# Attention and gated unit on one core: every step in a new written order, batch 0's q turned in row pairs, buffers given by number, ten more fillers on TensorE

## The chip, the core and the metric

The kernel runs on one core of a Trainium2 chip, in one launch. The metric is device time in microseconds (us), lower is better. All data are float32; the three weights of the gated unit arrive as float64 and are narrowed on the core.

## What is computed

The reference, cut to what matters (8 batches, 8 heads, 576 tokens, 64 numbers per head; model width 512; 5 taps):

```
kv   = einsum('bhsd,bhse->bhde', k, v)            # no softmax
out  = einsum('bhsd,bhde->bhse', q, kv)
x    = out / sqrt(mean(out*out, -1) + 1e-6) * g_norm      # then heads side by side: (8, 576, 512)
gate = sigmoid(sum over 5 taps of conv_w[tap] * x shifted by tap)
y    = (gate * (x @ w_val)) @ w_out
```

## The kernel before

The kernel has no loops of its own. A string `PLAN` names 1235 steps with their arguments, and the last lines of the kernel call one small function for each step, in that order. Each function issues a few instructions on a fixed engine, so the string is the order of every engine's queue at once: TensorE (PE) for products, VectorE (DVE), ScalarE (ACT), GpSimd (POOL), and SyncE (SP) for most of the transfers. An engine works its own list in order and waits at the first instruction whose operands are not there. The framework adds the waits.

One batch goes through these steps:

- `load_half k|v b i` (L302) and `load_q`, `load_q_rows` (L313, L327) fetch. For batch 0 the v halves and one half of q go out on ACT's queue, the rest on SP's.
- `turn_q_rows b j` (L471, batches 0 and 1): q lies token by token, and the products need it with the 64 numbers of a head along the partitions. A product with the identity turns one row of 64 numbers for four heads; two of these (upper and lower four heads, r = 0, 1) go to the two halves of the output's partitions. j counts groups of four rows of tokens, and the fifth group has two, so a batch takes 36 such products. `sort_q` (L481) copies the turned rows from the PSUM bank to `qT`, with ACT. Later batches use VectorE's own transpose instead (`turn_q`).
- `kv_product b i` (L432): k times v for half i, 36 products of 64x64. `kv_copy` (L445) puts the sums into SBUF; for batch 0 into the blocks of a block-diagonal matrix `kv_bd`, four copies with ACT.
- `raw_whole` (batch 0, L506) or `raw_pair`, `raw_tail`: q times kv, chunk by chunk of 128 tokens.
- `square` (ACT), `sums` (DVE, a reduction), `powers` (POOL, the inverse root), `normalise` (DVE for batch 0, ACT later): the root-mean-square norm.
- `turn_x`, `keep_x` (PE, ACT), or later `turn_blocks`, `move_blocks` (DVE, then transfers): x with the width along the partitions, in `xT`.
- `gate_start` (ACT), four `gate_tap` (DVE), `gate_end` (ACT, sigmoid), `gated` (DVE): the gate. `val_product` and `keep_val` for batches 0 and 1, `x_sums`, `val_fast` and `val_keep` for the rest: x times w_val. `token_sums`, `fast_product`, `fast_keep` and `out_product`, `keep_out`: the last product; `store` writes.

Beside batch 0, `narrow_weight` turns each 64-bit weight block into float32 in eight steps (five on DVE, three on ACT). `w_val` has four blocks, `w_out` four, and the taps with g_norm one (`cw`); `turn_cw` (PE, L412) and `keep_cw` (DVE, L416) finish the last. `start_warm 36` (L427) gives PE 36 small products with the identity before q arrives; nothing reads them.

Buffers come from rotating pools: a name such as `ot` has three, and each new tile takes the next one. PSUM has eight banks in one rotation:

```
def ps(shape, name):
    return psum.tile(shape, FP32, tag="bank", bufs=8, name=name)
```

Of the kernel before, what the change touches and what calls it, by code (L numbers as in the profile page):

```python
# [10 lines left out]
U32 = mybir.dt.uint32  # L11
# [8 lines left out]
load_q_rows 0 1; stage_weight cw 0; load_q_rows 0 0; load_half v 0 0; load_half k 0 0; narrow_weight cw 0 5;  # L20
narrow_weight cw 0 6; narrow_weight cw 0 0; load_half v 0 1; load_half k 0 1; narrow_weight cw 0 1;
narrow_weight cw 0 2; warm_up; stage_weight wval 1; stage_weight wval 0; start_warm 36; turn_q_rows 0 3;
turn_q_rows 0 2; turn_q_rows 0 0; kv_product 0 0; turn_q_rows 0 1; sort_q 0 0; sort_q 0 1; narrow_weight cw 0 3;
narrow_weight cw 0 4; narrow_weight cw 0 7; turn_q_rows 0 4; turn_cw; keep_cw; kv_product 0 1; sort_q 0 4;
sort_q 0 3; kv_copy 0 0; kv_copy 0 1; narrow_weight wval 1 5; narrow_weight wval 1 0; sort_q 0 2; raw_whole 0 3;
load_q_rows 1 1; narrow_weight wval 1 1; narrow_weight wval 1 6; narrow_weight wval 1 2; raw_whole 0 4;
raw_whole 0 2; load_q_rows 1 0; narrow_weight wval 0 0; narrow_weight wval 0 5; square 0 3; stage_weight wval 3;
narrow_weight wval 0 6; narrow_weight wval 1 3; sums 0 3; load_half k 1 0; square 0 2; square 0 4;
narrow_weight wval 0 1; narrow_weight wval 1 4; sums 0 2; narrow_weight wval 0 2; raw_whole 0 0; raw_whole 0 1;
powers 0 3; sums 0 4; narrow_weight wval 1 7; normalise 0 3; square 0 1; square 0 0; sums 0 1; sums 0 0;  # L30
turn_q_rows 1 2; turn_q_rows 1 0; turn_q_rows 1 3; narrow_weight wval 0 3; sort_q 1 0; turn_x 0 3;
turn_q_rows 1 4; sort_q 1 2; turn_q_rows 1 1; keep_x 0 3; narrow_weight wval 3 0; load_half v 1 0;
stage_weight wval 2; load_half k 1 1; load_half v 1 1; powers 0 2; sort_q 1 3; normalise 0 2;
narrow_weight wval 3 1; narrow_weight wval 0 4; normalise 0 4; narrow_weight wval 0 7; narrow_weight wval 3 5;
stage_weight wout 1; load_q 2 0; stage_weight wout 0; powers 0 1; turn_x 0 4; narrow_weight wval 3 2;
turn_x 0 2; load_half k 2 0; kv_product 1 0; load_q 2 2; stage_weight wout 2; normalise 0 0; normalise 0 1;
narrow_weight wval 3 3; keep_x 0 2; keep_x 0 4; narrow_weight wval 3 4; narrow_weight wval 2 0; turn_x 0 0;
narrow_weight wval 3 6; turn_x 0 1; val_product 0 1 1; keep_x 0 0; kv_product 1 1; keep_x 0 1;
narrow_weight wval 3 7; narrow_weight wval 2 5; gate_start 0 0; val_product 0 3 1; gate_start 0 3;
narrow_weight wval 2 1; halo 0; sort_q 1 4; kv_copy 1 1; sort_q 1 1; kv_copy 1 0; gate_start 0 1;  # L40
narrow_weight wval 2 2; raw_pair 1 3; gate_tap 0 0 3; gate_tap 0 0 2; gate_tap 0 3 3; narrow_weight wval 2 3;
gate_tap 0 3 2; gate_tap 0 0 1; narrow_weight wout 1 0; narrow_weight wout 1 5; narrow_weight wval 2 6;
narrow_weight wval 2 4; load_half v 2 0; load_half k 2 1; load_q 2 1; square 1 3; narrow_weight wout 1 1;
narrow_weight wout 1 2; raw_tail 1; load_half v 2 1; keep_val 0 1 1; val_product 0 0 0; square 1 2;
narrow_weight wval 2 7; keep_val 0 3 1; gate_tap 0 3 1; sums 1 3; gate_tap 0 0 0; narrow_weight wout 0 0;
gate_tap 0 1 3; sums 1 2; turn_q 2 0; powers 1 3; keep_val 0 0 0; gate_end 0 0; val_product 0 2 1;
val_product 0 0 1; powers 1 2; load_q 2 3; narrow_weight wout 1 3; square 1 4; normalise 1 3; sums 1 4;
narrow_weight wout 1 6; narrow_weight wout 1 4; gate_tap 0 1 2; keep_val 0 0 1; val_product 0 1 0; raw_pair 1 1;
normalise 1 2; powers 1 4; turn_x 1 3; square 1 0; val_product 0 2 0; narrow_weight wout 1 7; gated 0 0;
gate_tap 0 1 1; keep_val 0 1 0; normalise 1 4; narrow_weight wout 0 1; sums 1 0; gate_start 0 2; turn_x 1 4;  # L50
turn_x 1 2; val_product 0 3 0; square 1 1; keep_x 1 4; keep_x 1 3; keep_x 1 2; narrow_weight wout 0 5;
gate_tap 0 3 0; val_sums 0; narrow_weight wout 2 5; narrow_weight wout 2 0; powers 1 0; gate_tap 0 2 3;
gate_tap 0 2 2; narrow_weight wout 0 2; gate_tap 0 2 1; sums 1 1; narrow_weight wout 0 3; keep_val 0 2 0;
keep_val 0 3 0; keep_val 0 2 1; stage_weight wout 3; narrow_weight wout 0 4; narrow_weight wout 0 6;
gate_tap 0 1 0; narrow_weight wout 2 6; gate_end 0 3; kv_product 2 0; normalise 1 0; powers 1 1;
val_product 1 0 1; halo 1; val_product 1 1 1; kv_product 2 1; turn_x 1 0; normalise 1 1; keep_val 1 0 1;
turn_q 2 2; narrow_weight wout 0 7; gate_tap 0 2 0; gate_end 0 1; gate_end 0 2; val_sums 1; turn_q 2 1;
gated 0 3; gated 0 2; turn_x 1 1; val_product 1 3 1; load_q 3 0; keep_x 1 0; turn_q 2 3; load_q 3 1;
load_half v 3 0; load_half v 3 1; narrow_weight wout 2 1; kv_copy 2 1; keep_x 1 1; weight_sums 0; val_sums 2;
gate_start 1 1; val_product 1 1 0; kv_copy 2 0; keep_val 1 1 1; narrow_weight wout 2 2; gate_tap 1 1 3;  # L60
keep_val 1 3 1; narrow_weight wout 2 3; narrow_weight wout 3 0; raw_pair 2 3; narrow_weight wout 3 5;
gate_tap 1 1 2; gated 0 1; square 2 2; square 2 3; keep_val 1 1 0; gate_start 1 0; narrow_weight wout 3 1;
raw_pair 2 1; val_product 1 0 0; narrow_weight wout 3 2; val_product 1 3 0; narrow_weight wout 3 3;
narrow_weight wout 3 6; token_sums 0 0 0; sums 2 3; val_product 1 2 1; val_product 1 2 0; powers 2 3; sums 2 2;
turn_q 3 0; token_sums 0 0 1; narrow_weight wout 3 4; square 2 1; keep_val 1 0 0; keep_val 1 3 0; load_q 3 3;
narrow_weight wout 3 7; narrow_weight wout 2 4; narrow_weight wout 2 7; load_half k 3 0; load_q 3 2;
load_half k 3 1; powers 2 2; fast_product 0 0 0; sums 2 1; normalise 2 3; token_sums 0 0 2; turn_blocks 2 3;
normalise 2 2; square 2 0; turn_q 3 1; powers 2 1; gate_start 1 3; fast_product 0 1 0; fast_product 0 0 1;
fast_keep 0 0 0; keep_val 1 2 0; normalise 2 1; weight_sums 1; raw_tail 2; sums 2 0; gate_tap 1 0 3;
fast_keep 0 0 1; fast_product 0 0 2; fast_keep 0 0 2; powers 2 0; square 2 4; keep_val 1 2 1; fast_keep 0 1 0;  # L70
weight_sums 2; token_sums 0 0 3; fast_product 0 0 3; fast_product 0 0 5; turn_blocks 2 2; turn_blocks 2 1;
sums 2 4; fast_keep 0 0 5; gate_tap 1 0 2; normalise 2 0; fast_product 0 0 4; fast_product 0 1 2; powers 2 4;
fast_keep 0 1 2; store 0 0; normalise 2 4; turn_blocks 2 0; move_blocks 2 0; move_blocks 2 2; move_blocks 2 1;
kv_product 3 0; fast_keep 0 0 4; turn_q 3 2; gate_tap 1 0 1; gate_tap 1 0 0; weight_sums 3; turn_q 3 3;
fast_product 0 1 4; turn_x 2 4; fast_product 0 1 1; kv_product 3 1; keep_x 2 4; kv_copy 3 0; kv_copy 3 1;
fast_product 0 0 6; move_blocks 2 3; raw_pair 3 3; raw_pair 3 1; gate_tap 1 3 3; load_half v 4 0; load_q 4 0;
gate_end 1 0; fast_keep 0 1 1; square 3 3; fast_keep 0 0 6; square 3 1; fast_product 0 1 3; fast_product 0 1 5;
gate_tap 1 3 2; gated 1 0; fast_keep 0 1 4; gate_tap 1 1 1; val_fast 2 0 0; sums 3 3; sums 3 1; gate_tap 1 1 0;
fast_keep 0 1 5; square 3 0; fast_product 0 1 6; square 3 2; sums 3 2; x_sums 2 0; gate_end 1 1; val_fast 2 1 0;
powers 3 3; x_sums 2 1; x_sums 2 3; gate_tap 1 3 1; gate_tap 1 3 0; val_fast 2 0 1; val_keep 2 0 0;  # L80
val_fast 2 0 2; x_sums 2 2; val_sums 3; sums 3 0; gated 1 1; fast_keep 0 1 6; val_keep 2 1 0; normalise 3 3;
val_keep 2 0 2; powers 3 2; powers 3 1; gate_end 1 3; val_fast 2 1 2; val_fast 2 1 1; load_half k 4 0;
val_keep 2 1 2; gate_start 1 2; val_keep 2 0 1; val_fast 2 0 4; gate_tap 1 2 3; val_keep 2 1 1; gate_tap 1 2 2;
val_fast 2 1 4; val_fast 2 0 5; val_fast 2 1 5; load_half v 4 1; normalise 3 2; load_half k 4 1; val_keep 2 0 4;
turn_blocks 3 2; val_keep 2 1 4; turn_q 4 0; val_keep 2 1 5; store 0 1; load_q 4 1; store 0 3; gate_tap 1 2 1;
# [763 lines left out]
```

## Time and profile before

| What | Value |
|---|---|
| Runs | 306.4, 304.68, 305.18 us; median 305.18 |
| Profiled execution, span from first to last instruction | 304.6 us |
| PE busy | 294.8 us, 97%, 3441 matmul records |
| DVE busy | 269.2 us, 88%, 474 instructions |
| ACT, POOL busy | 193.7 us (64%), 114.9 us (38%) |
| HBM read, written | 39.21 MB, 9.44 MB |

The profile doesn't say which of the runs, if any, is the profiled one; what lies around its span isn't recorded. The span is 0.1 us under the fastest run and 0.6 us under the median.

How to read it: a float32 product on PE shows as two matmul records, a transpose as one. "Busy" of PE counts a record's whole latency, so neighbours overlap, and the distance from one to the next tells the rate. The chain of waits is followed back from the last instruction; where it stays on PE, PE was never kept waiting. The granted clock (PEclk) is known only from the first clock record on; ahead of that the page prints full.

### The profile page before, as it was taken

To read this page: it belongs to the slowest core of one execution; us is meant where nothing else is said; L and a number is where in the kernel's file an instruction comes from. 1 tells how busy PE (TensorE), PEld (TensorE's weight loads), DVE (VectorE), ACT (ScalarE), POOL (GpSimd) and SP (SyncE) were. 2 spreads that over 40 slices of the span, in tenths; PEclk is the share of its full clock that TensorE was granted. 3 is DMA by queue.
4 is the path that set the end of the run, shared out by engine and by line. 5 is a ranking of instruction groups with operands and counts; after the bars stand their busy time and mean duration, and the time that the engine had idled before them with its cause. 6 is when DMAs were issued, how large, how long until landed. Compare 5 with 4: busy or idle time off the path is not lost.

```text
span 304.6 us, 8977 instructions
## 1 busy us (share of the span) xinstructions
PE 294.8 (97%) x3441; PEld 232.4 (76%) x3441; DVE 269.2 (88%) x474; ACT 193.7 (64%) x596; POOL 114.9 (38%) x127
## 2 busy tenths in 40 slices
PE   7899999999999999999999999999999999999993
PEld 7788778877787785777778757787878588888582
DVE  1169999999999999999999999999999999999612
ACT  1569989999768664884586547683787354535220
POOL 3027354406568217364338352345536631000000
PEclk9979999999999999999999999999999999999999
DMA  7999998088569756988689477927411621112423
GB/s 269 343 368 343 272 302 210 4 230 269 154 147 329 231 163 167 269 220 260 173 253 294 111 175 232 326 72 214 114 48 30 169 80 34 36 42 64 103 69 103
DMA packets 32074, 55.53 MB, mean 182 GB/s; under 512 B 6166, under 2 KB 14358, under 8 KB 32032
## 3 DMA queue, kind: packets, MB, share of 16 engines
q1 hardware_dynamic: 29520, 49.76, 55.7%
q0 software_dynamic: 1632, 3.17, 4.1%
q10 hardware_dynamic: 880, 2.03, 1.8%
q8 instruction: 27, 0.44, 0.6%
q14 instruction: 15, 0.12, 0.1%
HBM read 39.21 MB, written 9.44 MB: 160 GB/s over the span
## 4 chain that ended last, share of the span: by engine, by line
PE 89%; DVE 5%; DMA 2%; issue 1%; ACT 1%; DVEq 0%; ACTq 0%; SPq 0%
PE a L774 18%; PE cb L774 14%; PE va L682 13%; PE val L633 11%; PE vc L682 6%; PE kvps L440 6%; PE raw L501 5%; PE out L720 5%; PE vb L682 4%; PE qTps L477 4%; PE raw L512 2%; PE xTps L583 2%; DMA qs<-in_q_dram 2%; DVE gate L621 2%; DVE xs L667 1%
## 5 line engine op out<-in xcount | busy, mean ns | idle before, releaser
L552 POOL TENSOR_TENSOR rt<-ss,mhalf 128x8 f32<-128x8 f32 (+3 forms) x38 | 68.9, 1822 | 101.0 <-DVE ss L544 100.8
L621 DVE SCALAR_TENSOR_TENSOR gate<-xT,cwT,gate 128x576 f32<-128x576 f32 x128 | 101.8, 809 | 1.0
L571 ACT ACTIVATE x<-raw,rt 128x64 f32<-128x64 f32 x252 | 55.8, 351 | 7.2 <-POOL rt L552 4.2
L604 POOL DMA_DIRECT2D xT<-y x48 | 26.4, 557 | 25.5 <-DVE ot L784 14.0
L633 PE MATMUL val<-xT,wval 128*128 128x288 f32 x128 | 33.0, 411 | 0.0
L774 PE MATMUL a<-wsum,sums 128*128 128x256 f32 x128 | 32.4, 382 | 0.0
L628 ACT ACTIVATE gate<-gate 128x576 f32<-128x576 f32 x32 | 22.0, 692 | 11.7 <-DVE gate L621 11.4
L633 PEld LDWEIGHTS val<-xT,wval 128*128 128x128 f32 x128 | 23.5, 190 | 6.5 <-ACT xT L590 0.4
L544 DVE TENSOR_REDUCE ss<-sq 128x8 f32<-128x520 f32 (+1 forms) x40 | 24.7, 627 | 2.9 <-ACT sq L531 2.5
L774 PEld LDWEIGHTS a<-wsum,sums 128*128 128x128 f32 x128 | 24.0, 190 | 4.1 <-issue 0.6
L535 ACT ACTIVATE sq<-raw 128x256 f32<-128x256 f32 (+1 forms) x70 | 22.4, 403 | 7.3 <-PE raw L501 7.1
L682 PE MATMUL va<-xs,vsum 128*128 128x288 f32 x96 | 26.6, 409 | 0.0
L615 ACT ACTIVATE gate<-xT,cwT 128x576 f32<-128x576 f32 x32 | 25.2, 811 | 1.5 <-DVE gv L646 1.3
L646 DVE TENSOR_TENSOR gv<-gv,gate 128x576 f32<-128x576 f32 x32 | 23.6, 750 | 0.9 <-ACT gate L628 0.8
L682 PEld LDWEIGHTS va<-xs,vsum 128*128 128x128 f32 x96 | 18.0, 190 | 5.1 <-ACT x L571 0.4
L611 POOL COPY xT<-xT 128x124 f32<-128x124 f32 x32 | 17.5, 585 | 10.5 <-ACT xT L590 10.5
L501 PEld LDWEIGHTS raw<-kv,qT 64*64 64x64 f32 x1008 | 16.4, 134 | 5.3 <-issue 3.0
L440 PEld LDWEIGHTS kvps<-v,k 64*64 64x64 f32 x1008 | 15.9, 135 | 3.7 <-issue 1.9
L501 PE MATMUL raw<-kv,qT 64*64 64x64 f32 x1008 | 18.7, 221 | 0.0
L440 PE MATMUL kvps<-v,k 64*64 64x64 f32 x1008 | 17.6, 220 | 0.0
L774 PE MATMUL cb<-wsum,sums 128*128 128x256 f32 x64 | 16.9, 386 | 0.1
L774 PE MATMUL cb<-wout,gv 128*128 128x256 f32 x64 | 16.8, 385 | 0.0
(111 smaller groups left out, 542.3 us busy)
## 6 DMA issues: line engine op xcount, KB each, us to landing
qs<-in_q_dram SPq DMA_DIRECT2D x96, 140.0 KB, 4.2
out_dram<-ot SPq DMA_DIRECT2D x140, 64.0 KB, 1.7
k<-in_k_dram SPq DMA_DIRECT2D x14, 576.0 KB, 6.3
v<-in_v_dram SPq DMA_DIRECT2D x12, 576.0 KB, 6.5
xT<-y SPq DMA_DIRECT2D x48, 64.0 KB, 2.7
xT<-y POOLq DMA_DIRECT2D x48, 64.0 KB, 3.3
y<-in_moe_w_val_dram SPq DMA_DIRECT2D x4, 512.0 KB, 11.4
w_wout<-in_moe_w_out_dram SPq DMA_DIRECT2D x4, 512.0 KB, 6.3
```

The costliest lines, as they stand in the source:

```text
L440: nc.tensor.matmul(st["kvps", b][s][r * D:(r + 1) * D, i], st["k", b, i][rows, r, cols], st["v", b, i][rows, r, cols], start=(j == 0), sto ...
L501: nc.tensor.matmul(st["raw", b, c][r][cols, to * D:(to + 1) * D], st["qT", b][rows, hp, first:first + D], kvs[b % 2][rows, hp, :], start=T ...
L544: nc.vector.reduce_sum(out=st["ss", b][:, FIRST[c]:FIRST[c] + n], in_=st["sq", b, c][:, 0:n], axis=AX.X)
L552: nc.gpsimd.tensor_tensor(out=st["rt", b][:, which], in0=st["ss", b][:, which], in1=mhalf[:, which], op=ALU.pow)
L571: nc.scalar.activation(out=x[:, to * D:(to + 1) * D], in_=raw[:, h * D:(h + 1) * D], func=AF.Copy, scale=root[:, to:to + 1])
L604: (nc.sync if i % 2 else nc.gpsimd).dma_start(out=xTs[b % 2][i * TB:(i + 1) * TB, :, first:first + P], in_=y[a * TB:(a + 1) * TB, i])
L615: nc.scalar.activation(out=gate[:], in_=xTs[b % 2][:, jt, HALO:SX], func=AF.Copy, scale=cwT[:, K - 1, jt:jt + 1])
L621: nc.vector.scalar_tensor_tensor(out=gate[:], in0=xTs[b % 2][:, jt, tap * TB:tap * TB + S], scalar=cwT[:, tap, jt:jt + 1], in1=gate[:], op ...
L633: nc.tensor.matmul(val[:], wval[:, kc, jt * P:(jt + 1) * P], xTs[b % 2][:, kc, HALO + n * SV:HALO + (n + 1) * SV], start=(kc == 0), stop=( ...
L646: nc.vector.tensor_tensor(out=both, in0=both, in1=st["gate", b, jt][:], op=ALU.mult)
L682: nc.tensor.matmul(st[bank, "val", b, mj][:], weights_[:, k], tokens()[:, k], start=(n in (0, 1, 3) and k == 0), stop=(k == NK // 2 - 1), ...
L774: nc.tensor.matmul(st[bank, i, p], tokens()[:, k], weights_[:, k], start=(n < 2 and k == 0), stop=(k == NK // 2 - 1), skip_group_check=True)
```

## The change

The diff replaces the whole string `PLAN` (1235 steps by 1238; the same steps with the same arguments, but for `start_warm`), and it does this in the functions:

- Buffers are no longer pools. Each name has fixed tiles (`ROOMS`), and a step says after an @ which of them its new tiles take. Names and sizes are those of before.
- Batch 0's q is turned by two rows of tokens at a time with a real transpose (128 numbers, two rows of 64, become 128 partitions), 18 instead of 36 operations. The result has the two rows on the two halves of the partitions, so `sort_q` of batch 0 has four copies instead of one, two with ACT and two with DVE.
- `kv_copy` of batch 0 gives two of its four copies to DVE.
- `start_warm` has a width: 36 products of 38 columns instead of 32 before q arrives, and 3, 6 and 1 of 256 columns further on.

By the built programs, PE goes from 1745 products to 1737 (36 row products out, 18 transposes and 10 fillers in), DVE from 476 instructions to 488, ACT from 598 to 601.

The string's beginning, before and after, and the functions:

```diff
-load_q_rows 0 1; stage_weight cw 0; load_q_rows 0 0; load_half v 0 0; load_half k 0 0; narrow_weight cw 0 5;
-narrow_weight cw 0 6; narrow_weight cw 0 0; load_half v 0 1; load_half k 0 1; narrow_weight cw 0 1;
-narrow_weight cw 0 2; warm_up; stage_weight wval 1; stage_weight wval 0; start_warm 36; turn_q_rows 0 3;
-turn_q_rows 0 2; turn_q_rows 0 0; kv_product 0 0; turn_q_rows 0 1; sort_q 0 0; sort_q 0 1; narrow_weight cw 0 3;
-narrow_weight cw 0 4; narrow_weight cw 0 7; turn_q_rows 0 4; turn_cw; keep_cw; kv_product 0 1; sort_q 0 4;
-sort_q 0 3; kv_copy 0 0; kv_copy 0 1; narrow_weight wval 1 5; narrow_weight wval 1 0; sort_q 0 2; raw_whole 0 3;
...
+load_q_rows 0 1; load_q_rows 0 0; load_half v 0 1 @ 0; load_half k 0 1 @ 0; start_warm 36 38 @ 0;
+load_half v 0 0 @ 0; load_half k 0 0 @ 0; stage_weight wval 1; stage_weight wval 0; stage_weight cw 0 @ 0;
+turn_q_rows 0 4 @ 1; turn_q_rows 0 1 @ 0; turn_q_rows 0 2 @ 2; turn_q_rows 0 3 @ 3; turn_q_rows 0 0 @ 4;
+start_warm 3 256 @ 5; load_q_rows 1 1; load_q_rows 1 0; narrow_weight cw 0 5 @ 0; narrow_weight cw 0 0 @ 0;
+stage_weight wval 3; kv_product 0 1 @ 6 7; narrow_weight cw 0 6 @ 1; narrow_weight cw 0 1; load_half k 1 1;
+narrow_weight cw 0 2; load_half v 1 1; warm_up; sort_q 0 4 @ 0; sort_q 0 2; start_warm 6 256 @ 5; sort_q 0 1;
+stage_weight wout 1 @ 1; narrow_weight cw 0 3; narrow_weight cw 0 4; narrow_weight cw 0 7; sort_q 0 0;
+sort_q 0 3; stage_weight wval 2; kv_product 0 0; turn_cw @ 4; start_warm 1 256 @ 5; load_half v 1 0;
+kv_copy 0 0; kv_copy 0 1; narrow_weight wval 1 5 @ 1; raw_whole 0 3 @ 3; narrow_weight wval 1 0 @ 0;
...
+    ROOMS = {"w64": (3, 1024), "ot": (3, 512), "wexp": (2, 512), "gate": (3, 576), "xs": (4, 576), "x": (2,
...
+    def new(tag, shape, dtype, name):
+        room = rooms[tag][picked.pop(0)]
...
     def ps(shape, name):
-        return psum.tile(shape, FP32, tag="bank", bufs=8, name=name)
+        return new("bank", shape, FP32, name)
...
-    def start_warm(n):
+    def start_warm(n, width):
+        reps = -(-width // P)
+        bank = ps([TB, reps, width // reps], f"warm{n}")
         for _ in range(n):
-            nc.tensor.matmul(warm_bank()[0:TB, 0, 0:TB], ident[:, 0:TB], ident[:, 0:TB], start=True, stop=True)
+            nc.tensor.matmul(
+                bank[0:TB], ident[:, 0:TB], ident[:, 0:width // reps].unsqueeze(1).broadcast_to((P, reps, width // reps)),
+                start=True, stop=True)
...
     def kv_copy(b, s):
         ps_ = st["kvps", b][s]
         if b in WHOLE:
             for r in range(2):
                 rows = slice(r * D, (r + 1) * D)
-                nc.scalar.copy(
+                (nc.vector.tensor_copy if r else nc.scalar.copy)(
...
     def turn_q_rows(b, j):
         m = min(HB, NB - j * HB)
-        pq = ps([P, HB, P], f"qTps{b}_{j}")
+        st["pq", b, j] = pq = ps([P, HB, P], f"qTps{b}_{j}")
+        if b in PAIRED_Q:
+            for r in range(2):
+                for n in range(0, m, 2):
+                    nc.tensor.transpose(
+                        pq[:, r * 2 + n // 2, :],
+                        qs[:, r, j * HB + n:j * HB + n + 2, :].rearrange("p n d -> p (n d)"), ident[:])
+            return
...
     def sort_q(b, j):
...
+        if b not in PAIRED_Q:
+            nc.scalar.copy(out=qT[:, j * HB:j * HB + m], in_=pq[:, 0:m])
+            return
+        for r in range(2):
+            for e in range(2):
+                (nc.vector.tensor_copy if b == 0 and e else nc.scalar.copy)(
+                    out=qT[r * D:(r + 1) * D, j * HB + e:j * HB + m:2],
+                    in_=pq[e * D:(e + 1) * D, r * 2:r * 2 + m // 2])
```

`PAIRED_Q` is (0,). Of batch 1 only the order changes.

## Prediction

> **What bounds it now.** I read the page's first and fourth part, then sums over stretches, then the chain's beginning in order of time.
>
> ```profile
> PE 294.8 (97%) x3441; PEld 232.4 (76%) x3441; DVE 269.2 (88%) x474; ACT 193.7 (64%) x596; POOL 114.9 (38%) x127
> ...
> PE 89%; DVE 5%; DMA 2%; issue 1%; ACT 1%; DVEq 0%; ACTq 0%; SPq 0%
> ```
>
> PE is the chain. By stretches (columns: stretch, then busy time and count of PE, PEld, DVE, ACT, POOL; then clock, DMA share, GB/s):
>
> ```profile
> 15.84:22.80 6.96, 6.40 (x84) 5.51 (x76) 4.47 (x10) 5.14 (x12) 1.87 (x1) 0.75 1.02 386
> 22.80:284.00 261.20, 260.31 (x3049) 204.12 (x3049) 256.44 (x432) 179.86 (x567) 110.64 (x118) 1.00 0.62 177
> 23.50:299.60 276.10, 275.10 (x3112) 214.42 (x3112) 261.24 (x440) 182.21 (x574) 110.40 (x117) 1.00 0.60 171
> ```
>
> From 23.5 to 299.6 PE stands idle for 1.0 us in all, and DVE, up to 284, for under 5. Both are full, so the new order can win little there. What is left is the beginning:
>
> ```profile
> 6.12 5.05 PE qTps L477 x48
> 11.17 1.21 PE kvps L440 x72
> 12.38 1.49 PE qTps L477 x24
> 13.86 1.19 issue
> 15.05 0.21 PE cwps L414
> 15.26 1.28 PE kvps L440 x67
> ...
> 17.15 6.32 PE raw L512 x40
> 23.47 2.77 PE qTps L477 x48
> ...
> 30.30 1.02 PE xTps L583 x8
> 31.32 1.70 PE val L633 x7
> ```
>
> Two things are to be seen. PE waits 1.2 us at 13.86 for the taps, and 0.6 more ahead of raw. And equal work takes two lengths: 48 records of q's turning 5.05 us at 6.12, 2.77 us at 23.47. The first are at half clock (105 against 58 ns a record), though the page prints full there, where no clock record exists. The later drop is on record (columns: stretch, PE, clock, DMA, GB/s):
>
> ```profile
> 10.50:13.90 3.40, 3.34 (x107) 1.00 1.06 377
> 13.90:17.30 3.40, 1.69 (x74) 1.00 0.77 253
> 17.30:20.80 3.50, 3.50 (x18) 0.51 1.01 374
> ```
>
> PE half idle for 3.4 us, then half clock for 3.4 us: that made raw 1.7 us longer.
>
> **What doesn't change.** The steps are the same, so PE's dense work is. Each step between 64x64 products (kv, raw) and whole-array ones costs PE 0.18 to 0.2 us (L774 x4 takes 1.06 us behind kv, 0.86 behind its like); both lists have 29 such blocks. Fixed buffers add no instruction; a wait that they add or remove counts in the last term below.
>
> **The beginning, step by step.** Times are on the profile's scale.
>
> *Transfers.* q lands at 6.1 and 6.25. The two k and v halves are only swapped: v lands 8.3 and 12.1 us after issue at 1.2 and 1.7, so 9.5 and 13.8; k's second at 13.6. SP's next loads, batch 1's q, waited for q's turning and went out at 13.88; then DMA ran at 0.77 of its time (row above). Now they can go at about 8.5, so what follows lands some 1 us earlier. w_val, k and v of batch 1 keep ahead of their uses; I take 0 for them.
>
> *Turning.* 36 products, 6.5 us with both clocks, become 18 transposes at 0.11 to 0.13 us (8 in 1.02), 2.0 us at full clock. The warm-up of 38 columns runs 38/32 as long as the old (4.05 us), 4.8, so to about 6: next to no gap ahead of q, where 0.7 us stood. With PE busy from 1.4 on I take full clock from about 7, so turning ends at 8.6. Three fillers of 256 columns (0.43 each, L774) end at 9.9, kv 0 1 at 11.2, six fillers at 13.8, just as k and v land; kv 0 0 at 15.1, `turn_cw` and the last filler at 15.7. So the fillers cost nothing if the clock is up. If it isn't, they push kv back (the second rival).
>
> *Copies.* ACT: 10 copies, 0.25 to 0.3 each; it is free of the table load at 11.2 and through with them and the taps' third step at about 14.2. DVE: 10 copies of 64x256 from PSUM. No row has one; 0.33 (L784's 256-column pace) is one end, 0.42 (L797 alone) the other: 3.3 to 4.2 us, of which six lie in a stretch that was idle (8.45 to 14.36: 5.25 us in one wait). The other four sit behind `narrow_weight cw 0 7`, which waits for ACT, at 13.8: through at 15.1 to 15.5. I take 0.33, the pace of a full queue. Behind those DVE has two kv copies, then w_val's narrowing, for which everything later waits. kv's four copies took 1.09 us on ACT alone; in twos beside each other 0.5. So raw starts at 15.7 instead of 17.15, and DVE at 15.6 instead of 15.84. Bounds: 15.6 to 16.3.
>
> *Raw to the first val.* Raw takes 4.45 at full clock (records 112 ns apart at its end), so to 20.15, against 23.47: 3.3 us gained. DVE's list, added up in its new order, stays fed: narrowing 5 steps and `keep_cw` to 18.5, then sums and narrowing by turns (0.60, 0.34, 0.65, 0.70 each); x of chunk 3 at 22.2, 4 at 25.0, 2 at 25.6, 0 and 1 at 28.2 and 28.8. In the old list 2.6 us of waits for `square` stood between 15.84 and 23. PE now comes first at the turning of x: its waits there are 0.3, 0.4 and 0.6. With turning (2.8 + 1.5), kv 1.4, x 2.0 the first val begins at 29.5, against 31.32. **The lead is 1.8 us**, not 3.3: DVE has the rest.
>
> *Later.* DVE gains once more. A `gate_tap` right behind one on the same gate waits for its result (first row: two gates; second: one gate):
>
> ```profile
> 272.42 1.54 DVE L621 SCALAR_TENSOR_TENSOR gate<-xT,cwT,gate 128x576 f32<-128x576 f32 x2
> ...
> 280.44 1.66 DVE L621 SCALAR_TENSOR_TENSOR gate<-xT,cwT,gate 128x576 f32<-128x576 f32 x2
> ```
>
> 0.12 us each. Instructions of DVE that read the one just ahead of them: 50 in the old list, 32 in the new, so 2.2 us less on DVE. That is cover for PE, not time: PE has only its 1.0 us of idle time, and some restarts behind it, to win. I take 0.4 of that. New waits at other places can cost: from 0 up to one whole handoff from square to x (0.58 + 0.70 + 2.06 + 0.68 = 4.0, rows L531, L544, L552, L561); I take 0, as DVE's lead over PE has grown, and keep both ends. The tail behind `out_product 3 8` has the same 26 half products and stores: 0.
>
> **Sum.** 304.6 - 1.8 - 0.4 = 302.4 on the profiled execution's scale. The median of the runs lies 0.6 higher, so 302.9.
>
> **Rivals.**
>
> *All of DVE's lead arrives.* DVE's 2.9 us at the start (2.6 of waits, 0.24 of start) and all idle time of PE: 304.6 - 2.9 - 1.0 = 300.7, 301.2 as a median. For it: DVE is full. Against: PE has no such slack.
>
> *The fillers run at half clock: slower.* The clock was still half at 10.5 in the old kernel, with 72 warm-up records and some 40 of q behind it; transposes may do still less to raise it. Then turning takes 3.8 us (to 10.0), three fillers 2.6 (to 12.6); with full clock from 13.9, one stretch of 3.4 us of products later, kv 0 1 ends at 14.5, the six fillers, which now stand in front of k and v that have landed, at 17.1, kv 0 0 at 18.5, and raw begins at 19.0. Raw ends where it did (23.45), but DVE's narrowing starts 3.3 us later than I forecast, so the first val comes at 32.8, 1.4 later than before: 306.0, 306.4 as a median. It decides when full clock comes after about 11.5; later than 13.9, up to 1 us more. The Trainium skill (TensorE: Matmul & The Clock Gate, part 4, PE-mode transpose) says that transposes don't count as work for the clock; by that rule this rival holds. No run yet shows a stretch of them.
>
> *The lead is lost later.* An order is only as good as the times it was planned with. A handoff 1.8 us short, under half of the 4.0 chain, uses it up: 304.6, 305.1 as a median. For it: PE and DVE are both full, so nothing makes up for it. Against: DVE's extra 2.2 us.
>
> *It does not do what it says.* The fillers are real work for PE, as the lists show, so this could only be the clock, above.
>
> **Chances.** Forecast 0.45 (302.9, spread about 1 us), DVE's whole lead 0.12, lost later 0.23, half-clock fillers 0.20. About 0.5% (1.5 us, 303.7 and 306.7) is what a measurement can tell from no change. Faster: 0.12 and five sixths of 0.45, 0.50. Same: the rest of the forecast, the lost lead, and half of the fillers' case, 0.36 with a little off for worse handoffs. Slower: 0.14. The range takes in both ends: 300.9 to 306.4.
>
> **What would show it.** Full clock ahead of the first kv and none below it until the end; kv 0 0 at about 13.8; raw at 15.7, 4.45 us long; w_val's narrowing at 15.6 and DVE without a wait for `square`; the first val at 29.5. Wrong, if kv 0 0 starts behind fillers after k and v have landed, if PE waits for DVE between 30 and 284 by more than 1 us, or if DVE has idle time there while PE is busy with what it waits for.

## The result, and the profile after

| | before | after |
|---|---|---|
| Median of 6 runs each (lowest to highest) | 305.47 us (304.68 to 306.4) | 315.58 us (313.98 to 317.85) |
| Ratio | | 1.034 [1.030, 1.038] |
| Span of the profiled execution | 304.6 us | 314.5 us |
| First val product begins | 31.32 us | 32.65 us |
| PE idle from raw's end to the end of its dense work | 1.0 of 276.1 us | 9.6 of 285.7 us |

Slower by 10 us, where 2.3 faster was forecast. Two rows hold it all: the first val product comes 1.3 us later, and PE then stands idle for 8.6 us more. 1.3 + 8.6 = 9.9, the difference of the spans. Before's trace is that of its longest run (306.4 us; every run with both numbers lies about 1.8 us above its span), after's that of a run 0.7 us above the median.

The page of after, the lines that answer to the first ones of before (busy time, and the chain of waits by engine):

```profile
PE 296.4 (94%) x3407; PEld 231.8 (74%) x3407; DVE 272.0 (86%) x486; ACT 195.9 (62%) x599; POOL 112.7 (36%) x127
...
PE 54%; DMA 17%; DVE 14%; SPq 8%; issue 3%; ACT 2%; POOL 1%; DVEq 0%; POOLq 0%; ACTq 0%
```

PE's busy share fell only from 97 to 94%, but the chain left PE: from 89% to 54%. DMA, DVE and SP's issuing (SPq) now hold 39% of it. That is how a kernel looks whose busiest engine is kept waiting. By stretches (stretch; busy time and count of PE, PEld, DVE, ACT, POOL; granted clock, DMA share, GB/s):

```profile
6.20:8.50 2.30, 2.24 (x19) 2.07 (x20) 0.26 (x2) 0.00 (x0) 0.00 (x0) 1.00 1.05 398
...
14.60:18.20 3.60, 1.46 (x35) 0.86 (x33) 2.64 (x9) 1.89 (x7) 0.00 (x0) 1.00 1.02 387
...
18.70:22.10 3.40, 3.40 (x20) 3.18 (x20) 3.27 (x10) 2.46 (x5) 0.00 (x0) 0.50 1.06 387
...
24.40:310.10 285.70, 276.06 (x3112) 215.40 (x3112) 259.39 (x439) 183.55 (x573) 108.04 (x117) 1.00 0.57 163
```

The transposes of q (first row) run at full clock: it is granted from 5.04 us on. Then PE works for 1.46 of 3.6 us, and half clock follows for 3.4 us, as it did before; raw again takes 6.2 us. The last row is the dense stretch, with its 9.6 us of idle time.

The beginning's chain in order of time (start, length, what; the numbered buffers make every PSUM tile a "bank"):

```profile
13.94 0.37 ACT qT L531
14.31 0.02 issue
14.33 0.43 DVE qT L531
...
16.16 0.43 DVE qT L531
16.58 0.03 issue
16.61 0.44 DVE qT L531
17.05 0.02 issue
17.07 0.37 ACT qT L531
17.45 0.02 issue
17.47 0.43 DVE qT L531
17.90 0.22 DVE kvbd L484
18.11 0.04 issue
18.16 6.22 PE bank L559 x40
...
32.65 0.49 PE bank L680 x2
```

`sort_q`'s copies (L531) of one bank run in single file: ACT, DVE, ACT, DVE. Only the first copy of a bank runs beside the last one of the bank ahead (four times in 20 copies). So raw (L559) starts at 18.16, later than the old 17.15, and not at 15.7.

What PE waited for, in all (us in total, times, longest):

```profile
PE bank L729 <- DMA xT<-y: 2.2, 2, 1.4
PE bank L474 <- DMA qs<-in_q_dram: 2.2, 1, 2.2
PE bank L474 <- issue: 1.4, 1, 1.4
...
PE bank L729 <- ACT x L618: 1.2, 1, 1.2
PE bank L820 <- DVE ot L830: 0.9, 1, 0.9
PE bank L474 <- DMA k<-in_k_dram: 0.8, 1, 0.8
PE bank L820 <- ACT ot L834: 0.7, 1, 0.7
...
PE bank L820 <- ACT ot L836: 0.6, 1, 0.6
```

No single wait is the loss. Transfers (x's moves, k and v) stand for 5.2 us of it, `ot` for 2.2. L474 is the kv product, which reads k and v and not q: at 107 it waits for semaphores 103 and 108, which v (issued at 99.37) and k (issued at 102.30, landed at 108.83) raise; a q load is on one of the two as well, which is how the wait got its name. In the chain:

```profile
92.53 0.77 SPq L356
93.30 0.05 issue
93.36 6.00 DMA qs<-in_q_dram
99.36 0.02 issue
99.37 5.21 DMA v<-in_v_dram
104.58 0.02 issue
104.60 4.38 DMA qs<-in_q_dram
108.98 1.27 PE bank L474 x72
```

From 93.36 on one transfer follows another with 0.02 us between them, all on SP's list (the last, too, is k and not q). In the trace SP's transfers go round eight semaphores, and one waits until the last one on its semaphore, most often eight issues earlier, has landed. k's issue stood behind a q load that waited until 101.47 for the v load of 94.74. A load of k takes 6.5 us to land (median), so a load that stands behind others goes out late however free its buffer is.

### The profile page after: what moved, and what is told of

Read it like the earlier page. It is cut to its first block, busy times and chain, and to the rows that moved or that the text cites. A ratio compares the mean times of both kernels' runs of the same rounds, so it can differ in the third digit from the quotient of the medians.

```text
span 314.5 us, 8915 instructions
## 1 busy us (share of the span) xinstructions
PE 296.4 (94%) x3407; PEld 231.8 (74%) x3407; DVE 272.0 (86%) x486; ACT 195.9 (62%) x599; POOL 112.7 (36%) x127
## 4 chain that ended last, share of the span: by engine, by line
PE 54%; DMA 17%; DVE 14%; SPq 8%; issue 3%; ACT 2%; POOL 1%; DVEq 0%; POOLq 0%; ACTq 0%
PE bank L820 17%; PE bank L729 12%; PE bank L680 10%; DMA qs<-in_q_dram 6%; DMA v<-in_v_dram 4%; PE bank L474 4%; DVE gate L668 4%; PE bank L767 3%; SPq L852 3%; DMA xT<-y 3%; PE bank L548 3%; SPq L651 2%; PE bank L559 2%; DVE gv L693 2%; DMA w<-in_moe_conv_w_dram 2%
## 5 line engine op out<-in xcount | busy, mean ns | idle before, releaser
L668 DVE SCALAR_TENSOR_TENSOR gate<-xT,cwT,gate 128x576 f32<-128x576 f32 x128 | 100.5, 808 | 0.6
L618 ACT ACTIVATE x<-bank,rt 128x64 f32<-128x64 f32 x252 | 56.2, 366 | 10.3 <-POOL rt L599 7.1
L820 PE MATMUL bank<-wsum,w 128*128 128x256 f32 x192 | 47.3, 382 | 0.6 <-ACT ot L836 0.6
L820 PEld LDWEIGHTS bank<-wsum,w 128*128 128x128 f32 x192 | 36.0, 190 | 7.3 <-ACT ot L836 1.0
L729 PE MATMUL bank<-xs,vsum 128*128 128x288 f32 x144 | 39.2, 410 | 0.0
L680 PE MATMUL bank<-xT,wval 128*128 128x288 f32 x128 | 33.2, 410 | 0.0
L820 PE MATMUL bank<-wout,gv 128*128 128x256 f32 x128 | 32.7, 383 | 0.0
L729 PEld LDWEIGHTS bank<-xs,vsum 128*128 128x128 f32 x144 | 26.8, 190 | 7.1 <-DVE xs L714 0.2
L582 ACT ACTIVATE sq<-bank 128x256 f32<-128x256 f32 (+1 forms) x70 | 20.9, 372 | 15.2 <-PE bank L548 15.1
L729 PE MATMUL bank<-xT,wval 128*128 128x288 f32 x96 | 26.3, 411 | 4.1 <-DMA xT<-y 2.2
L680 PEld LDWEIGHTS bank<-xT,wval 128*128 128x128 f32 x128 | 23.5, 190 | 6.0
L820 PEld LDWEIGHTS bank<-wout,gv 128*128 128x128 f32 x128 | 23.9, 190 | 4.1 <-ACT ot L834 0.4
L729 PEld LDWEIGHTS bank<-xT,wval 128*128 128x128 f32 x96 | 17.7, 190 | 9.7 <-DVE gate L668 1.8
L474 PEld LDWEIGHTS bank<-v,k 64*64 64x64 f32 x1008 | 16.2, 135 | 10.6 <-issue 7.3
L474 PE MATMUL bank<-v,k 64*64 64x64 f32 x1008 | 18.2, 221 | 4.5 <-DMA qs<-in_q_dram 2.2
```

The lines of the kernel that those rows point to most:

```text
L474: nc.tensor.matmul(st["kvps", b][s][r * D:(r + 1) * D, i], st["k", b, i][rows, r, cols], st["v", b, i][rows, r, cols], start=(j == 0), sto ...
L618: nc.scalar.activation(out=x[:, to * D:(to + 1) * D], in_=raw[:, h * D:(h + 1) * D], func=AF.Copy, scale=root[:, to:to + 1])
L668: nc.vector.scalar_tensor_tensor(out=gate[:], in0=xTs[b % 2][:, jt, tap * TB:tap * TB + S], scalar=cwT[:, tap, jt:jt + 1], in1=gate[:], op ...
L680: nc.tensor.matmul(val[:], wval[:, kc, jt * P:(jt + 1) * P], xTs[b % 2][:, kc, HALO + n * SV:HALO + (n + 1) * SV], start=(kc == 0), stop=( ...
L729: nc.tensor.matmul(st[bank, "val", b, mj][:], weights_[:, k], tokens()[:, k], start=(n in (0, 1, 3) and k == 0), stop=(k == NK // 2 - 1), ...
L820: nc.tensor.matmul(st[bank, i, p], tokens()[:, k], weights_[:, k], start=(n < 2 and k == 0), stop=(k == NK // 2 - 1), skip_group_check=True)
```

## The experiments

Ratios are to the kernel before, run on the same chip. "Late idle" is PE's idle time behind 34 us in the profiled execution: 0.9 in before, 9.6 in after.

### Which half of the change

**Theory**: the new order's handoffs behind the first val product are too short. **Rivals**: the fixed buffers add waits; or the late start upsets the rest.

new_order_pools:

```diff
-        room = rooms[tag][picked.pop(0)]
+        t = (loads if tag in ("w64", "k0", "k1", "v0", "v1") else work).tile(
+            shape, dtype, tag=tag, bufs=ROOMS[tag][0], name=name)
```

> The changed kernel's order and code, but with the old rotating pools in place of buffers by number. If the order is what costs (theory: transfers wait in SyncE's queue and land late), it stays near 315 us, within 2. If the fixed buffers add the waits (rival), it falls to within 3 us of the kernel before, 305 to 308.

314.88 us, 1.030 [1.023, 1.036]; late idle 6.5, and 3.4 us of half clock at 110.4, which after's trace hasn't. The buffers' numbers are not the cause; the order is.

new_start_old_rest and old_start_new_rest, both with pools:

```diff
 PLAN: changed kernel's steps up to val_product 0 1 1
-then the changed kernel's order
+then the remaining steps in the old order
```

> The new order up to the first val_product, then all remaining steps in the old order; new code, rotating pools. If the start alone is 1.3 us late and the rest of the old order gives nothing back: 306.5 to 307. If the start's delay is the seed of everything later (rival): 310 or more.

308.31 us, 1.010 [1.007, 1.013], between the two expectations; late idle 1.1. The edit leaves `kv_product 1 0` ahead of the first val product, where before and after have one kv product there and this kernel two (1.2 us); the kernels named start_by_banks, which are made from it, have this too.

```diff
-PLAN, PAIRED_Q, kv_copy and start_warm of the changed kernel up to val_product 0 1 1
+those of the kernel before
 then the remaining steps in the new order
```

> The old order and old code up to the first val_product, then all remaining steps in the new order, rotating pools. If the loss lies in the later order: 313 to 315, 8.6 us over before. If it is seeded by the late start (rival): about 306.

314.11 us, 1.029 [1.019, 1.038]; late idle 7.1. So the halves are two separate losses: about 9 us behind the first val product, some 3 in the start (3.4 and 9.2; together 2.6 more than the whole, so they overlap). The late start does not cause the late waits.

### The place of the transfers

**Theory**: loads stand too far back in SP's list.

new_order_loads_early:

```diff
-load_half and load_q of batch 3 and later where the plan has them
+each right behind the step that frees its buffer
```

> The changed kernel with the loads of k and v from batch 3 on, and of q, moved up in the order to right behind the step that frees their buffer; nothing else moves. If PE's waits of 2.2 and 0.8 us come from loads that stand too far back in SyncE's queue, both vanish and the time falls by 3 us or more, to 312 or less. If the transfers are slow by themselves or the waits have another cause: 315, unchanged.

351.99 us (353.72 with a fourth run of 358.3), 1.155 [1.144, 1.165]: wrong by 40 us. What PE waited for there:

```profile
PE bank L718 <- DMA xT<-y: 14.3, 5, 6.0
PE bank L537 <- DVE qT L486: 13.3, 3, 5.4
```

As I read it, the large k and v loads fill the eight places, and the short transfers behind them, x's moves and q, land late. That theory fell in its simple form: it isn't "too late" but "in the wrong turn".

new_order_old_transfers and old_order_new_transfers give the list of one order to the other:

```diff
 PE, DVE, ACT, POOL: new order
-SP's steps where the new order has them
+SP's steps in the old relative order, each as early as its data and its turn allow
```

> The changed kernel (with rotating pools), and behind the first val product only SP's list is put back: loads, moves of x and stores follow one another as in the kernel before, each as early as its data allow (two loads and one store go one to three places ahead, since the new order needs them sooner); PE, DVE, ACT and POOL keep the new order. If the new order of the transfers is what made PE wait, the gaps behind 100 us go and the time is 306 to 309 us (new_start_old_rest has 308.3). If the lists of PE, DVE and ACT are themselves too tight, PE still waits for 9 us in all and the time stays at 313 or above.

373.42 us, 1.222 [1.218, 1.227]; neither theory had such a loss in it.

> The mirror image: the kernel before, the new code's buffers from pools and its turning of q with the old written order up to the first val product; behind it PE, DVE, ACT and POOL keep the old order, and SP's list follows the new one. If the transfers' order alone costs, this is slower than before by 5 us or more (311 to 317 us). If not, it is within 2 us of the kernel before (303.5 to 307), as the old lists leave the time for it.

344.55 us, 1.127 [1.122, 1.133]: slower, as the first theory said, but by 39 us and not 5 to 12. PE's waits in new_order_old_transfers (the second line, at 153, is a kv product that waits for k, on semaphore 108):

```profile
PE va L704 <- DMA xT<-y: 17.8, 3, 7.2
PE kvps L449 <- DMA out_dram<-ot: 7.9, 1, 7.9
PE raw L523 <- DVE qT L472: 5.5, 1, 5.5
PE kvps L449 <- DMA k<-in_k_dram: 5.3, 1, 5.3
```

Neither list is bad in itself: with its own order the old one leaves 0.9 us of late idle time. But SP's list works in order. A transfer at its head that waits for a late step of another engine stops those behind it: SP's waits for `ot` from DVE add up to 70.8 us in new_order_old_transfers, against 27.1 in after and 43.3 in before. Two lists that don't belong together cost 39 and 68 us.

new_order_k_v_first:

```diff
+load_half v 4 0 @ 0; load_half k 4 0 @ 0;
 load_half k 4 1 @ 0; ... load_half v 4 1 @ 0; ... store 0 0;
-load_half v 4 0 @ 0; ... load_half k 4 0 @ 0;
```

> The changed kernel with two loads moved: v and k of batch 4, first half, which kv 4 0 needs, go ahead of the second half's k in SP's list (they went out behind it, two q loads and a store, and landed at 108.8, when PE had waited 2.2 us). If the wait is a matter of their place, PE's gap at 107 goes, and the time falls by up to 2.2 us (313 to 314); if SP is short of issue time as a whole, another wait (kv 4 1, q, or x's moves behind it) takes its place, and the time stays within 1 us of the changed kernel's 315.6 or rises.

313.72 us (314.91 with a fourth run of 318.07, the one that was profiled), 1.030 [1.024, 1.035]. No gain is shown: the interval overlaps after's, and the times don't tell the two expectations apart. In the trace PE's wait of 2.2 us at 107 is gone, so that one was a matter of place. The next batch's kv waits 2.95 us at 143.6, where it waited 0.8 in after: its k, issued at 138.75 (138.27 in after), took 7.6 us to land and not 6.5.

### What of the stores is in the way

**Theory**: in the new order SP's list has no room for the stores. **Rivals**: the lists of PE, DVE and ACT are too tight by themselves; or the stores hold the `ot` buffers.

new_order_few_stores and old_order_few_stores leave out the stores of the first three pairs of batches:

```diff
     def store(i, c, queue=nc.sync, blocks=range(HB)):
+        if i < 3:
+            return
```

> The changed kernel without the stores of the first three pairs of batches (that part of the output isn't written; only the last pair's is): 108 transfers fewer in SP's list, and no ot buffer waits for a store. If PE's later waits (9.5 us behind 40 us) come from transfers that stand behind stores in SP's list or from ot buffers that a store holds, they shrink to under 4 us and the time is 307 to 310 us. If the lists of PE, DVE and ACT are too tight in themselves, it stays at 313 to 316.

307.97 us, 1.011 [1.006, 1.015].

> The control: the kernel before without the same stores. PE has 1.0 us of idle time to lose behind 23 us, so 303.5 to 305.5 us by either theory; a fall of more than 2 us would mean that the stores cost something that isn't PE's idle time, such as DMA traffic beside its work.

304.03 us, 0.998 [0.995, 1.000]. By the ratios the same stores cost the new order about 7 us (1.034 to 1.011) and the old one half a microsecond. The dense stretch of new_order_few_stores:

```profile
24.40:302.00 277.60, 273.44 (x3092) 214.46 (x3086) 259.38 (x440) 182.33 (x573) 110.41 (x117) 1.00 0.50 142
```

PE idles for 4.2 us of it (1.3 of that ahead of 34 us), not 9.6, and PE, DVE and ACT have the very lists of after. So they aren't too tight by themselves, or only by 2 us (late idle 2.9 against 0.9).

new_order_small_stores and new_order_six_ot:

```diff
-            queue.dma_start(out=rows_out[2 * i + bb, n], in_=ot[j * TB:(j + 1) * TB, :])
+            rows = TB if i == 3 else 2
+            queue.dma_start(out=rows_out[2 * i + bb, n, 0:rows], in_=ot[j * TB:j * TB + rows, :])
```

> The changed kernel; each store of the first three pairs writes 2 of its 32 rows (the other 30 are left out): 4 KB instead of 64. The issues, their waits for ot and their places among the eight transfers in flight stay, the bytes go. If the stores cost through SP's list, 312 to 316 us as with whole stores. If through DMA's time or through ot buffers that a store holds for 1.7 us, 307.5 to 310 as without them.

311.17 us (309.0 to 311.98), 1.020 [1.014, 1.025]; between the two expectations.

```diff
-    ROOMS = {..., "ot": (3, 512), ...
+    ROOMS = {..., "ot": (6, 512), ...
```

> new_order_pools (314.9 us) with six ot buffers instead of three; all stores whole. If PE's later waits come from ot buffers that wait for their store, 308 to 311 us. If from loads and moves of x that stand behind stores in SP's list, 313 to 316, with the gap for batch 4's k at 107 to 109 still there.

314.65 us, 1.031 [1.026, 1.036], as new_order_pools; late idle 9.9. PE's first waits:

```profile
PE va L704 <- DMA xT<-y: 3.3, 3, 1.5
PE kvps L449 <- DMA out_dram<-ot: 3.3, 1, 3.3
```

The second line is once more kv's wait for k, issued at 138.34 and landed at 145.9; the gap at 107, which was expected to stay, is not there. The buffers are out. Of the 7 us, about 4.5 go with the bytes (ratio 1.034 to 1.020) and 2.8 with the issues and their waits in SP's list (1.020 to 1.011). The split is rough: the intervals of the two kernels touch, and in new_order_small_stores' trace, that of its shortest run (309.0), late idle is 3.2, next to 2.9 without the stores, so that there the bytes account for nearly all of it. Whether a byte costs by DMA traffic, or by holding one of the eight places for longer, stays open.

new_order_one_store, old_order_one_store, and new_order_one_store_banks, which also has the edit of start_by_banks below:

```diff
         ot = st["ot", i, c]
+        if len(blocks) == HB and c < 2 * NJ:
+            n = c % NJ * HB
+            queue.dma_start(out=rows_out[2 * i + c // NJ, n:n + HB], in_=ot[:])
+            return
```

> The changed kernel with one transfer of 256 KB for each store of four blocks of rows, in place of four of 64 KB: the same bytes, from the same places of the list, but 32 issues on SP instead of 128 (the two half products at each pair's end that are stored in other pieces stay as they are). If SP's time per issue (0.42 us) and its eight transfers in flight are what make loads and moves late, the later waits of PE shrink as without the stores: 308 to 311 us. If it is the bytes or the ot buffers, it stays at 313 to 317.

343.99 us, 1.126 [1.121, 1.132].

> The kernel before with the same edit of store. PE has under 1 us of waits behind 23 us and lost 0.5 us to all these stores, so 303.5 to 305.5 us by either theory; slower than 306 would mean that one large store holds its ot buffer longer than four small ones.

330.33 us, 1.083 [1.080, 1.087].

> new_order_one_store, and the start's copies by whole PSUM banks (groups 2 and 0 of q and the second kv bank to DVE, the rest to ACT). DVE's narrowing of w_val starts at 17.3 instead of 18.1 by start_by_banks_own_bank: if the start's lead carries through, 0.8 to 1.6 us below new_order_one_store; if later waits take it up, the same time.

344.82 us, 1.130 [1.126, 1.134].

The first expectation missed with both its values. The second holds by its last clause, one large store holds `ot` longer, and the third by "the same time". The reason is the edit's own. In old_order_one_store's chain one store takes this long:

```profile
208.30 7.64 DMA out_dram<-ot
...
220.84 7.86 DMA out_dram<-ot
```

Before, a store of 64 KB landed in 1.7 us (median), and four went side by side. While a single store was under way near the end, a quarter of the DMA engines was busy (second last column):

```profile
314.00:318.50 4.50, 4.50 (x23) 3.96 (x22) 0.26 (x1) 0.74 (x2) 0.00 (x0) 1.00 0.23 58
```

0.23 of 16 is 3.7. The Trainium skill (DMA: Bandwidth & Descriptors, section Why a DMA increments its semaphore by 16 and not by 1) says that a transfer is spread over the largest number of engines, 16 at most, that divides the slowest dimension of both its sides. Here that dimension is 4 on the output's side, where the four transfers of 32 rows each had 32; the trace agrees with 4 engines. The edit thus made `ot` scarce (ACT waits 40 us in all for a store to give one back, 5.7 in before), which is another experiment than was meant: it says nothing of SP's issue time. With rows of tokens as the slowest dimension it wasn't tried.

### The start

**Theory**: ACT and DVE wait for each other because both read the same PSUM bank. **Rivals**: they write stripes of the same partitions of `qT`; or PE's own pause in kv 0 0 sets the start.

start_by_banks (new_start_old_rest, with):

```diff
-                (nc.vector.tensor_copy if b == 0 and e else nc.scalar.copy)(
+                (nc.vector.tensor_copy if b == 0 and j in (2, 0) else nc.scalar.copy)(
 ...
-                (nc.vector.tensor_copy if r else nc.scalar.copy)(
+                (nc.vector.tensor_copy if s else nc.scalar.copy)(
```

> new_start_old_rest (308.3 us, first part new, the rest in the old order), with one edit: of the copies at the start, a whole PSUM bank goes to one engine (groups 2 and 0 of q and the second kv bank to DVE, the rest to ACT) in place of halves of each bank to either. In the built lists the waits of ACT and DVE for each other are gone. If two engines on one bank are what made the copies run one at a time, all are through by 14.5 to 15.5, raw starts at 15.5 to 16.5 instead of 18.2, the first val product 1.5 to 2.5 us earlier, and the time is 305.5 to 307. If PE's own pause of 1.4 us in kv 0 0 and the half clock set the start, raw starts at 17.3 or later and the time is 307.5 to 309.

306.73 us, 1.004 [1.002, 1.007]: 1.6 below new_start_old_rest. DVE's waits for ACT at q's copies, 4.4 us in after, are gone. Raw starts at 16.8 (forecast 15.5 to 16.5) and, at full clock throughout, takes 4.7 us. In the built lists the waits also stay if the engines are divided by upper and lower partitions of `qT`, and go if whole banks are: it is the bank that the framework orders, not the stripes.

start_by_banks_no_fillers:

```diff
-start_warm 3 256; ... start_warm 6 256; ... start_warm 1 256;
```

> start_by_banks without the ten products of 256 columns. If the fillers hold the clock up, PE's clock falls behind the 18 transposes, kv and raw run at half clock (raw 6.3 us instead of 4.5), and the time is 1 to 3 us above start_by_banks. If they only stand in the way of k and v, which land at 12.4, kv 0 0 starts 1.2 us earlier, the pause in it comes earlier or goes, and the time is 0 to 1.5 us below start_by_banks.

311.25 us, 1.018 [1.015, 1.022]: with the fillers it is 4.5 us less. Without them:

```profile
14.10:20.90 6.80, 5.27 (x35) 4.75 (x36) 6.50 (x18) 4.31 (x10) 0.06 (x1) 0.50 1.05 406
```

half clock for 6.8 us, over the whole of raw. And PE's pauses of the kind "issue", in which no semaphore holds it, have grown to four of about 1 us or more:

```profile
PE kvps L448 <- issue: 4.2, 3, 1.8
...
PE raw L522 <- issue: 1.3, 2, 1.0
```

start_by_banks_own_bank and start_by_banks_9_warm ask what these are:

```diff
-        bank = ps([TB, reps, width // reps], f"warm{n}")
+        if "warm" not in st:
+            st["warm"] = ps([P, C], "warm")
+        bank = st["warm"][0:TB, 0:width].rearrange("p (a b) -> p a b", a=reps)
```

> start_by_banks (306.7 us) with all warm-up products and fillers in one PSUM bank of their own, as the changed kernel gives them; in start_by_banks the six fillers waited 1.31 us for a bank that q's copies held. If PE's pause in kv 0 0 is the fetch of its instructions (in three traces PE stands still ahead of its instruction 449 until 1.35 to 1.41 us after a 16 KB instruction packet ends), the 1.3 us only change their place: fillers on time, then a pause of 1 to 1.5 us in kv 0 0, and the time is within 0.5 us of start_by_banks. If the pause was a matter of the copies, it is gone, raw starts at 15.5, and the time is 305.0 to 306.0.

306.44 us, 1.005 [1.003, 1.008]: the same as start_by_banks; PE's pause in kv 0 0 is back with 1.2 us.

```diff
-start_warm 36 38;
+start_warm 9 152;
```

> start_by_banks_own_bank with a warm-up of 9 products of 152 columns instead of 36 of 38: the same columns, 108 PE instructions fewer ahead of kv 0 0. If the pause is the fetch of instruction 449, it moves 54 records on, out of kv 0 0 into raw, whose products then begin 1 us earlier, or it goes, if the packet comes in time: 0 to 1.5 us faster than start_by_banks_own_bank. If the pause belongs to kv 0 0 (its data, or the banks), it stays behind record 42 of the 72, and the time stays.

311.02 us, 1.020 [1.016, 1.024]. The pause left kv 0 0, as the first expectation had it, but the time missed both: a longer pause came later, with half clock behind it.

```profile
PE kvps L451 <- issue: 2.2, 1, 2.2
```

The trace records PE's instruction packets: 27 of 16 KB for its 6,900 instructions, so 256 to a packet. The pauses against the packets:

| kernel | PE stands still ahead of its instruction | from, to (us) | packet ends | to PE's restart |
|---|---|---|---|---|
| after | 449 | 14.61, 16.05 | 14.64 | 1.41 |
| start_by_banks_own_bank | 449 | 14.54, 15.70 | 14.22 | 1.48 |
| start_by_banks_no_fillers | 449 | 13.55, 15.34 | 13.99 | 1.35 |
| start_by_banks_no_fillers | 961 = 449 + 2 x 256 | 32.34, 33.70 | 32.34 | 1.36 |
| start_by_banks_no_fillers | 1217 = 449 + 3 x 256 | 39.88, 40.84 | 39.46 | 1.38 |
| start_by_banks_no_fillers | 3265 = 449 + 11 x 256 | 110.99, 112.07 | 110.77 | 1.30 |
| start_by_banks_9_warm | 961 | 32.71, 34.94 | 33.46 | 1.48 |

In before, the packet ahead of instruction 449 ended at 11.27, four microseconds before its use. So PE waits for its program; the traces have no event of the fetch itself, but in these kernels the pauses of 1 us or more within one step's products all come at such an instruction. Why a packet is late is not settled. In after it went out 4.1 us after PE had passed instruction 193, in before 1.7; the DMA engines were busy with a share of 0.96 to 1.08 ahead of most of these pauses, but 0.56 ahead of the one at 111.

**What sets the first val product** can be read from two kernels made for the stores. new_order_few_stores has after's lists, and the clock stayed full: raw ended at 23.1, 1.3 us ahead of after's, and the first val still began at 32.55 (32.48 in after, in the same view); PE waits there for x from DVE three times, 1.2 us in all. So DVE sets it. old_order_few_stores has before's steps up to 80 us, and no half clock in the start:

```profile
14.50 0.43 DVE L380 TENSOR_SCALAR ot_wval<-y 128x512 uint32<-128x512 uint32 x1
...
15.67 4.96 PE L512 MATMUL raw<-kvbd,qT 128*128 128x128 f32 x40 [0.56 <-ACT kvbd L450]
...
28.56 2.11 PE L633 MATMUL val<-xT,wval 128*128 128x288 f32 x8
```

In before's trace these begin at 15.84, 17.15 and 31.16. So the old start is not always as slow as that trace shows it. Against this one after's first val comes 3.9 us later, not 1.3, which fits the 3.4 us that new_start_old_rest lost.

## Why the prediction was wrong, step by step

The sum was 302.4 on the span's scale; measured 314.5. Of the 12.1 us between, 3.1 lie ahead of the first val product (29.5 forecast, 32.65 measured) and 9.0 behind it (0.4 to be won, 8.6 lost).

- **Transfers**, taken as 0 up to the first val: right. k and v landed by 9.3 and 12.4, earlier than forecast. The step stopped there, with batch 1's loads; what failed stands under Later.
- **Turning**: right. 18 transposes took 2.2 us (2.0 forecast), the clock was full from 5.04. kv 0 0 began at 13.71 (13.8). Not forecast: PE's pause of 1.4 us in it, for instructions.
- **Copies**: failed, and with it the lead. I let ACT and DVE copy side by side. Each of q's banks is read by both, and within a bank the framework puts one behind the other. A copy of DVE took 0.43, not 0.33: the end of the bounds that I set aside. Raw started at 18.16 (bounds 15.6 to 16.3), and DVE's narrowing of w_val, behind the last kv copy, at 18.3, not 15.6.
- **Raw to the first val**: raw's 4.45 us at full clock was right as a price (4.7 in the runs by banks), but after's pauses brought the clock down once more. And the step took a lead of PE for one of the first val, which DVE sets. In start_by_banks_own_bank raw ended at 21.7, DVE's narrowing began at 17.28 and the first val at 32.56, of which 1.2 us are the kv product that stands behind it elsewhere. Without that it is 31.35, 2.8 us behind the old start at full clock (28.56), as DVE's narrowing is (14.50). Twelve more copies on DVE cost more than PE's shorter turning won. (The terms written for this step add up to 29.2, not 29.5.)
- **Later**: this is the term of 9 us. "New waits at other places" had the bounds 0 and 4.0, and I took 0 "as DVE's lead over PE has grown". DVE's gain was there, though smaller: `gate_tap` went from 101.8 to 100.5 us, 1.3 of the 2.2 forecast. But over half of PE's waits (5.2 of 9.3 us) are for transfers, which that argument didn't touch, and the bound of 4.0, one handoff from square to x, holds no transfer either. Without the stores of three pairs late idle falls from 9.6 to 2.9. I compared the lists of PE and DVE and did not price SP's: 34 `store` steps, loads of 6 us and x's moves, eight in flight, in a new turn. Whether the stores do it by their issues or by their bytes stays open.
- **The rival "fillers at half clock"** did not hold: the clock was full 6 us before its point of decision. The Trainium skill's rule on transposes (TensorE: Matmul & The Clock Gate, part 4) would have had the clock not rise through them; it had risen ahead of them, and 2.2 us of transposes did not bring it down, though PE did only 0.65 us of other work from 5.04 to 8.45 (it fell behind 3.4 us in which PE was busy for 1.93, from 15.28 on). "Lost later" was the right rival with a price of 1.8 us for what cost 8.6; it asked whether PE and DVE were full, not whether SP was.
- **The scale**: the profiled execution of before must be the run of 306.4 us, 1.8 above its span. I added 0.6, and in the sums only 0.4 to 0.5. That moves the sum by 1.2 and not by 12. It weighs more that this one trace has half clock in raw: I counted the 1.7 us of it as the new order's to win, and the old order's start is without it in old_order_few_stores.

No version that does the whole work beats the kernel before. The nearest whole ones, start_by_banks and start_by_banks_own_bank, are 0.4 and 0.5% slower.

## What to carry to other kernels

A reordering changes the list of the queue that issues the transfers too: read that list as an engine's, with its places in flight, its landing times and what its head waits for, ahead of counting any lead on the compute engines. A transfer that gives up its turn can cost more than any instruction, and moving a single pair of loads won nothing that could be measured. One trace of the kernel before is one execution: a clock drop in it is not a cost that every run pays. Where two engines are to share a PSUM bank's readers, look first whether the framework lets them run beside each other; whole banks to either engine do.

## What the runs showed of the hardware

- **PE can run out of instructions.** At instruction 449 and every 256 from there it stands still until 1.3 to 1.5 us after the 16 KB packet has ended, when that packet is late: 1.0 to 2.2 us a time, always among the 64x64 products of kv and raw in the table's cases. What makes the packet late stays open.
- **The clock moves by steps of 3.41 us.** Its records last whole multiples of 3.41 us (3.41, 6.83, 10.24, 13.65 and long ones), and a drop follows some pauses of PE and not others: in old_start_new_rest a pause of 2.6 us brought 3.4 us of half clock, in new_order_six_ot one of 3.3 us none. Ten fillers of 256 columns, whose results nothing reads, were worth 4.5 us, with the pauses that they kept away.
- **One store of 256 KB took 5.9 to 8.6 us** in nine of the ten places where old_order_one_store's chain waits for one, **four of 64 KB about 1.7 each**, side by side: one transfer with a slowest dimension of 4 kept a share of 0.23 of 16 DMA engines busy, about four.
